# A mixer block on one core: chunk 0's gate moved behind step two of chunk 1, q loaded last, w_mod in small loads, part of every chunk's kv on GpSimd

## The chip, the cores and the metric

The kernel runs on one core of a Trainium2 chip. The metric is device time in microseconds for one execution; the median of several runs is compared. The engines of a core work in parallel, each through its own list of instructions in the order in which the kernel's text issues them, and they meet only through semaphores: TensorE (PE in the profile; PEld are its weight loads), VectorE (DVE), ScalarE (ACT), GpSimd (POOL), and SyncE (SP), which here only issues transfers. ScalarE can issue transfers too (ACTq).

## The reference

Inputs are q, k, v (2048 tokens, 640 channels, float32), a conditioning vector c, and weights.

```python
mod = (silu(c) @ w_mod).reshape(c.shape[0], 6, 1, -1)
sa, ca, ga, sb, cb, gb = ...             # six rows of 640
h = layernorm(q) * (1 + ca) + sa
# A: short causal convolution of k (4 taps), times v, long causal convolution
#    with ssm_k (2048 taps per channel, by FFT) plus ssm_D, times h
k_shift = sum of k delayed by t, times shift_k[:, 3 - t], t = 0..3
kv = k_shift * v
y = irfft(rfft(kv, 2S) * rfft(ssm_k, 2S))[:S] + kv * ssm_D
x = q + ga * (h * y)
# B: token-mixing MLP
h = layernorm(x) * (1 + cb) + sb
u = gelu(einsum("bsd,sf->bdf", h, w1) + b1)
out = x + gb * (einsum("bdf,fs->bds", u, w2) + b2).transpose
```

## The kernel before

The first part, some 290 us, does A; the rest does B, and its text is the same in both kernels. The order of all work is written out by hand: a line in the text puts an instruction at the end of its engine's list, and nothing reorders it later.

The 640 channels are taken in five chunks (c = 0..4) of 128. The long convolution is a matrix form of a Fourier transform, with these steps per chunk:

- *kv*: `kv_ops(g)` computes k_shift times v for a quarter g of the tokens: 8 elementwise instructions of 128x512 (tiles `tap`, `kt`, result in `x`). On GpSimd the same 8 instructions use the tile `t` (`PS_`, `PT`, `PW`). `kv(c_next)` gives the instructions of all quarters for VectorE, and when a quarter is done it issues the loads of k and v for the chunk after (`kv_loads`); `fill` holds them and `dv(n)` puts the next n on VectorE.
- *step one*: `step1(side, t)`, t = 0..3. 32 matmuls each (L230); ScalarE copies the result to `z` (L235). Side 0 transforms kv, side 1 transforms ssm_k. Before side 1, `perm_add` (GpSimd) adds ssm_D to one row of ssm_k as loaded by `load_ks`, and `perm` (ScalarE, L177, result in `p`) reorders it.
- *step two*: `f2(g)`, g = 0..7. 64 matmuls (L249); ScalarE copies a half (L255, `kt`), VectorE multiplies the transforms (`p<-pst,kt`, two instructions per g, into one of two halves of `P`), GpSimd adds and subtracts the products (`y<-p`, two instructions per g). In the text, the products of g - 1 and the sums of g - 2 stand behind the matmuls of g. `perm_add` of the next chunk stands behind those at g = 3.
- *back*: `i2(r)`, r = 0, 1 (L280, four copies by ScalarE, L288), and `i1(half)` (L300).
- *gate*: `a1_ops` puts the normalised q, scaled, in `A1` (half of the tile `aux`; 16 rows by ScalarE, L307, then two VectorE instructions); `gate` multiplies `A1` by y from PSUM and adds it to q in `xa`, `xb` (`XH`); `spill` stores the result to DRAM.

PSUM is a ring of three tiles of 1024 (`psum()`), so every fourth user waits until the first was read; a fourth tile, `tap`, holds VectorE's kv scratch.

Stages: chunk 0's kv; step one of both sides, then step two of chunk 0; then a stage in which chunk c goes back and is gated while step one of chunk c + 1 runs, followed by step two of chunk c + 1, and so on. The modulation rows sa, ca, ga come from w_mod (five loads of 128 x 1920 by `mod_load`, products `mod_part` in TensorE, L364, `mod_sum`, and `mod_row`, L375); three rows give `G0`, `G1`. Chunk 0's gate needs them, and needs q with its row statistics (`bn_stats`, L600, and `rstd`).

In the stage behind chunk 0's step two, SyncE's list is: the 32 q loads (already issued in step two, L532), w_mod, the constants `c_v1` of i1, chunk 1's ssm_k (`load_ks(1)`), chunk 2's k and v, `load_taps(3)`, chunk 2's ssm_k (`load_ks(2)`), the stores of chunk 0's result. The w_mod pieces 0 to 4 lie in the tiles `v`, `aux` and `p`.

The stage of chunk c = 1, 2 or 3 in the text (ScalarE's part in brackets): two step ones of side 0 [copies], `perm(c + 1)` [one instruction], 7 kv instructions, `i2(0)` [4 copies], the two VectorE instructions of `a1_ops`, `step1(0, 2)`, `i2(1)`, `step1(0, 3)`, then `i1`, gates and step one of side 1. Chunk c's 16 rows of `a1_ops` are put on ScalarE in step two, two per g.

`copy_rows` copies parts of w1 from DRAM to DRAM (`wc`) for later use in B; these ten transfers are issued in step two of chunk 3.

## Time and profile before

| what | us |
| --- | --- |
| median of 3 runs (lowest, highest) | 672.45 (670.65, 674.04) |
| the profiled execution's own time | 671.21 |
| its span, first to last instruction | 669.4 |
| step two of chunk 0 | 41.4 to 57.7 |
| stage of chunk 0 (back and gate; step one of chunk 1) | 57.7 to 105.4 |
| step two of chunk 1 | 105.4 to 126.7 |
| stage of chunk 1 | 126.7 to 156.3 |
| step two of chunk 2 | 156.3 to 172.7 |
| stage of chunk 2 | 172.7 to 201.6 |
| step two of chunk 3 | 201.6 to 220.1 |
| stage of chunk 3, step two of chunk 4, last gate and norm | 220.1 to 344 |
| part B's matmuls | 344 to 669 |

In rows of the order of time the columns are: start in us, duration in us, engine, line, operation, output<-input, partitions x elements and type, xcount (neighbouring instructions of one kind are merged), and in brackets the idle time in front with what ended it. In rows of stages: the window, its length, then busy time (and count) of PE, PEld, DVE, ACT and POOL, the granted TensorE clock as a share of full speed, the busy share of the transfer engines, and GB/s.

### The profile page before, as it was taken

Reading aid. Unit: us, or ns where it says so; the run is one execution under the profiler, and the core shown is the slowest. Engines: PE = TensorE matmul, PEld = TensorE weight load, DVE = VectorE, ACT = ScalarE, POOL = GpSimd, SP = SyncE. Lnnn points to the kernel's source line nnn. Section 1 sums busy time; section 2 is a strip of 40 time slices with the busy share of each in tenths; the row PEclk is TensorE's granted clock in tenths of the full one; section 3 lists DMA queues with packets and bytes.
Section 4 is the critical chain, followed back from the end, with each engine's and each line's share of the span. In section 5 each row is a group of like instructions: output and inputs, shape, how many; then the busy total and the mean of one; then the engine's idle time right before and its main releaser. Section 6 shows DMA issues by size and latency. Waiting matters only on the chain.

```text
span 669.4 us, 20749 instructions
## 1 busy us (share of the span) xinstructions
PE 619.5 (93%) x9073; PEld 597.8 (89%) x9073; DVE 501.9 (75%) x860; ACT 309.7 (46%) x483; POOL 108.1 (16%) x120
## 2 busy tenths in 40 slices
PE   0599878899998999999999999999999999999997
PEld 0598568788997989689999999999999999999997
DVE  6688569969969948789974213846689889888886
ACT  0574475545735647667765224334243332333331
POOL 5284027413324127000000000000000000000000
PEclk9999789999999999879999999999999999999999
DMA  9968988727438525414006630885598565345601
GB/s 179 213 194 225 391 172 159 168 54 165 83 70 221 180 51 156 172 33 95 0 1 126 119 71 1 189 234 144 174 365 268 173 179 154 102 144 169 188 31 41
DMA packets 175472, 98.01 MB, mean 146 GB/s; under 512 B 89843, under 2 KB 165398, under 8 KB 175126
## 3 DMA queue, kind: packets, MB, share of 16 engines
q1 hardware_dynamic: 170834, 95.38, 54.0%
q10 hardware_dynamic: 4548, 1.31, 1.1%
q8 instruction: 71, 1.16, 0.7%
q14 instruction: 19, 0.16, 0.1%
HBM read 79.63 MB, written 19.14 MB: 148 GB/s over the span
## 4 chain that ended last, share of the span: by engine, by line
PE 71%; DVE 16%; DMA 6%; issue 3%; SPq 2%; ACT 1%; POOL 0%; ACTq 0%; DVEq 0%; POOLq 0%
PE pst L1128 26%; PE pst L463 19%; PE pst L230 9%; PE pst L249 7%; PE pst L280 5%; PE pst L993 4%; DVE tap L60 3%; DVE kt L60 2%; DMA aux<-in_A_ssm_k_dram 2%; PE pst L300 2%; DMA aux<-in_w_mod_dram 2%; DVE p L60 1%; SPq L532 1%; PE tap L364 1%; DMA in<-in_A_k_dram 1%
## 5 line engine op out<-in xcount | busy, mean ns | idle before, releaser
L249 PE MATMUL pst<-z,w 128*64 128x64 f32 x2560 | 78.9, 223 | 11.0 <-DVE p L60 6.0
L249 PEld LDWEIGHTS pst<-z,w 128*64 128x64 f32 x2560 | 76.8, 138 | 13.7 <-issue 10.4
L230 PE MATMUL pst<-v,x 128*64 128x128 f32 x640 | 45.7, 302 | 24.2 <-DVE x L60 23.7
L230 PEld LDWEIGHTS pst<-v,x 128*64 128x64 f32 x640 | 43.6, 221 | 24.9 <-POOL t L488 23.7
L235 ACT ACTIVATE z<-pst 128x1024 f32<-128x1024 f32 (+2 forms) x45 | 41.4, 931 | 43.6 <-PE pst L230 24.9
L60 POOL TENSOR_TENSOR y<-p 128x256 f32<-128x256 f32 x72 | 54.1, 776 | 40.1 <-DVE p L60 39.7
L60 DVE TENSOR_TENSOR p<-pst,kt 128x512 f32<-128x512 f32 x80 | 50.8, 681 | 10.5 <-ACT kt L255 9.6
L280 PEld LDWEIGHTS pst<-v,y 32*128 32x128 f32 x1280 | 39.4, 193 | 4.2 <-issue 2.7
L280 PE MATMUL pst<-v,y 32*128 32x64 f32 x1280 | 41.2, 279 | 1.6 <-issue 1.0
L255 ACT ACTIVATE kt<-pst 128x512 f32<-128x512 f32 x40 | 23.9, 598 | 36.7 <-PE pst L249 20.9
L230 PE MATMUL pst<-v,p 128*64 128x128 f32 x640 | 37.3, 274 | 1.4 <-ACT p L177 1.2
L230 PEld LDWEIGHTS pst<-v,p 128*64 128x64 f32 x640 | 35.3, 137 | 2.2 <-ACT p L177 1.4
L1128 PE MATMUL pst<-r_z,m_w 128*128 128x320 f32 x198 | 37.2, 309 | 0.0
L60 DVE TENSOR_TENSOR tap<-tap,kt 128x512 f32<-128x512 f32 x51 | 35.5, 696 | 1.3
L60 DVE TENSOR_TENSOR kt<-in,tap 128x512 f32<-128x512 f32 x51 | 34.9, 685 | 1.5
L300 PEld LDWEIGHTS pst<-z,v 64*64 64x64 f32 x1280 | 24.7, 157 | 7.9 <-issue 3.5
L1128 PEld LDWEIGHTS pst<-r_z,m_w 128*128 128x128 f32 x198 | 31.1, 188 | 0.0
L300 PE MATMUL pst<-z,v 64*64 64x64 f32 x1280 | 26.9, 243 | 3.7 <-issue 2.4
L288 ACT ACTIVATE z<-pst 128x512 f32<-128x512 f32 x38 | 21.3, 664 | 18.3 <-PE pst L280 18.3
L1065 ACT ACTIVATE m_w<-m_v 128x896 fp32r<-128x896 f32 x19 | 17.9, 948 | 23.3 <-DVE m_v L60 13.0
L60 DVE TENSOR_TENSOR m_w<-m_v,m_w 128x896 fp32r<-128x896 f32 x19 | 20.6, 1086 | 6.5 <-ACT m_w L1065 6.5
L1128 PE MATMUL pst<-h_x,m_w 128*128 128x320 f32 x132 | 24.6, 309 | 0.0
(303 smaller groups left out, 1417.2 us busy)
## 6 DMA issues: line engine op xcount, KB each, us to landing
x<-in_B_w_dram SPq DMA_DIRECT2D x18, 512.0 KB
m_v<-in_B_w_dram SPq DMA_DIRECT2D x20, 384.0 KB
aux<-in_A_ssm_k_dram SPq DMA_DIRECT2D x10, 512.0 KB
out_dram<-m_w SPq DMA_DIRECT2D x32, 160.0 KB
in<-in_A_k_dram SPq DMA_DIRECT2D x36, 128.0 KB
in<-in_A_v_dram SPq DMA_DIRECT2D x36, 128.0 KB
ts<-m_p SPq DMA_DIRECT2D x10, 320.0 KB
m_w<-xs SPq DMA_DIRECT2D x20, 160.0 KB
```

Source lines behind the costliest of these rows:

```text
L60: TT = lambda eng, o, a, b, op: eng.tensor_tensor(o, a, b, op=op)
L230: pe.matmul(ps.rearrange("p (b m a) -> p b a m", b=2, a=4)[64 * ri:64 * ri + 64, a // 4, a % 4], lhs, F1[:, 128 * ri:128 * ri + 128], star ...
L235: act.activation(Z[:, side, t, :, k0:k1], ps.rearrange("p (b k a) -> p b k a", b=4, a=4)[:, :, k0:k1], AF.Copy)
L249: pe.matmul(pk[64 * h:64 * h + 64, kk // 4, ri, kk % 4], W2[k1 // 32][:, 2 * (k1 % 32) + ri], rhs, start=True, stop=True)
L255: act.activation(halves_(kt), pv[:, :, 1], AF.Copy)
L280: pe.matmul(pp[qd // 2][:, o:o + 64], Y[p, ri, i:i + 2].rearrange("p i k -> p (i k)"), V2[p, 64 * ri:64 * ri + 64], start=ri == 0, stop=ri ...
L288: act.activation(o, i, AF.Copy)
L300: pe.matmul(ps[64 * b:64 * b + 64, 512 * e + 64 * jj:512 * e + 64 * jj + 64], V1[p, ri, n2], T2[p, :, 32 * ri + n2], start=ri == 0, stop=r ...
L463: pe.matmul(ps[0:m, h, 0:320], w_.bitcast(F32R), r_[:, 320 * h:320 * h + 320].bitcast(F32R), start=first and i == 0, stop=last and i == 2)
L993: pe.matmul(ps[n][:, h, 0:320], sets[n][:, j].bitcast(F32R), r[:, 320 * h:320 * h + 320].bitcast(F32R), start=j == 0 and r is hh, stop=j = ...
L1065: act.activation(W[n][0].bitcast(F32R), A[p, w_], AF.Copy)
L1128: pe.matmul(bank[n], w[:, i].bitcast(F32R), r.bitcast(F32R), start=m == 0 and k == 0, stop=m == 6 and k == 2)
```

## The change

1. *w_mod in small loads, early.* Pieces 0 to 2 go, as 18 loads of 64 x 640 (`mod_gently`), into `xa` and the front of `xb`, where q will lie later; they and `c_v1` are issued ahead of step one of chunk 0. Pieces 3 and 4 go into the rest of `xb`, behind the loads of chunk 2's k and v.
2. *q last.* The 32 loads of q are issued behind the five w_mod products, `xb` first. The statistics: five rows by VectorE ahead of chunk 1's side-1 step one, then, in step two of chunk 1 from g = 2, one row by VectorE (`q_stats`) and one by ScalarE (`q_moments`) per g. SyncE's list is now: w_mod (part), k and v of chunk 2, w_mod (rest), `load_ks(1)`, q, k and v of chunk 3, `load_ks(2)`.
3. *Chunk 0's gate behind step two of chunk 1.* In the stage of chunk 0, ScalarE stores y from PSUM in `aux` where `A1` lies. In the stage of chunk 1 come `rstd`, 16 rows by ScalarE (`late_rows`, into the tiles `t` and `kt`), three VectorE instructions and a GpSimd add per half (`late_gate`), the store of chunk 0, and then all 16 rows of chunk 1's `a1_ops` at once (`run(ac)`).
4. *kv.* In the stage of chunk 0, VectorE runs its three quarters of chunk 2's kv at once, in place of spreading them over step two of chunk 1. In the stages of chunks 1 and 2, quarter 2 of the next kv goes to GpSimd: seven instructions at the front, the last behind `step1(0, 3)`. VectorE has 24 instructions there in place of 32.
5. *Row copies.* They are issued at the ends of the stages of chunks 1 and 2.
6. *Tap loads* for chunks 2 and 3 are issued by ScalarE.

The diff, cut to its core:

```diff
+    def mod_gently(kk, place):
+        for j in range(3):
+            for b in range(2):
+                sync.dma_start(place[j][64 * b:64 * b + 64],
+                               dram(w_mod, (128 * kk + 64 * b) * 6 * D + 640 * j, [[6 * D, 64], [1, 640]]))
...
     all_taps()
-    load_taps(2)
+    xab = [XR(j) for j in range(8)] + [T_x[1][:, 0:640]]
+    pl = [xab[0:3], xab[3:6], xab[6:9]] + [...]
+    sync.dma_start(T_v1[:, 0:4096], c_v1, max_dma_last_dim=4096)
+    for kk in range(3):
+        mod_gently(kk, pl[kk])
...
+    def q_moments(j):
+        act.activation(T_t[:, 0:640], XR(j), AF.Identity, scale=1 / D, accum_out=mv[:, j, 0:1])
+        act.activation(tm[:, j:j + 1], mv[:, j, 0:1], AF.Copy, scale=-D ** -0.5)
+        act.activation(T_t[:, 640:1280], XR(j), AF.Square, scale=D ** -0.5, bias=tm[:, j:j + 1],
+                       accum_out=mv[:, j, 1:2])
+    def late_rows(half):
+        for i in range(8):
+            j = 8 * half + i
+            act.activation(G_[half][:, i], XR(j, 0, DC), AF.Identity, scale=rs1[:, j:j + 1], bias=nm1[:, j:j + 1])
+    def late_gate(half):
+        a = G_[half]
+        g = lambda G: G[:, None, 0:DC].to_broadcast([128, 8, DC])
+        TT(dve, a, a, g(G1), ALU.mult)
+        TT(dve, a, a, g(G0), ALU.add)
+        av = a.rearrange("p j (m e) -> p e j m", e=2)
+        y = T_aux[:, 2048 + 1024 * half:3072 + 1024 * half]
+        TT(dve, av, y.rearrange("p (e j m) -> p e j m", e=2, j=8), av, ALU.mult)
+        x = XH[half][:, :, 0:DC]
+        TT(pool, x, x, a, ALU.add)
...
-            if c:
+            if c > 1:
                 n_ = 2 if cn is not None else 3
                 for f_ in ac[n_ * g:n_ * g + n_]:
                     f_()
-            if cn == NC - 1:
-                copy_rows(2, g % 2, g // 2, 1)
-                if g in (3, 6):
-                    copy_rows(3, g // 6)
...
             if c == 0 and g < 4:
                 lay_w2(1, g)
-                if g == 3:
-                    load_q()
+                if g == 1:
+                    load_taps(2, act)
+            if c == 1 and g > 1:
+                q_stats(QJ[2 * g + 1])
+                if g < 7:
+                    q_moments(QJ[2 * g + 2])
...
             if c and cn is not None and g == 3:
                 perm_add(cn)
...
         if c == 0:
+            pool.tensor_scalar(PW, TR.rearrange("p (i s) -> p s i", s=4), 1.0, None, op0=ALU.mult)
+            taps()
+            load_taps(3, act)
             load_k(2, 1)
...
             load_v(2, 3)
+            for kk in (3, 4):
+                mod_load(0, kk, T_x[1][:, 1920 * kk - 4480:1920 * kk - 2560])
+            load_ks(1)
+            for t in range(4):
+                step1(0, t)
             perm_add(1)
             run(kv_ops(2, pool))
+            ps = psum()
+            pe.transpose(ps[:, 0:36], stg, ID[0:36, 0:36])
+            act.activation(cols, ps[:, 0:36], AF.Copy)
+            act.activation(sil, cols[:, 30:35], AF.Silu)
+            i2(0)
+            i2(1)
+            ps = psum()
+            for kk in range(5):
+                mod_part(ps, kk, pl[kk])
+            load_q()
+            mod_sum(ps, T_kt[:, 0:640])
             perm(1)
+            ops = kv(3, ((0,), (1, 2), (3,)))
+            run(ops)
             load_ks(2)
         elif cn is not None:
+            if c == 1:
+                rstd(rs1, nm1, 0, 16)
+            step1(0, 0)
+            if c == 1:
+                late_rows(0)
+            step1(0, 1)
+            if c == 1:
+                late_rows(1)
+                for half in range(2):
+                    late_gate(half)
+                spill(0)
+                run(ac)
             perm(cn)
             if c + 2 < NC:
-                fill.extend(kv(c + 3 if c + 3 < NC else None))
+                pool_ops = kv_ops(2, pool)
+                run(pool_ops[:-1])
+                fill.extend(kv(c + 3 if c + 3 < NC else None, ((0,), (1, 2), (3,))))
...
             step1(0, 3)
+            if cn < NC - 1:
+                run(pool_ops[-1:])
             dv(3 if cn < NC - 1 else 28)
...
         for half in range(2):
             ps = i1(half)
+            if c == 0:
+                act.activation(T_aux[:, 2048 + 1024 * half:3072 + 1024 * half], ps, AF.Copy)
+                if half:
+                    for i in range(3):
+                        mod_row(i, T_kt[:, 0:640])
+                    for j in QJ[0:5]:
+                        q_stats(j)
+                continue
...
+        if c:
+            spill(c)
+        if c in (1, 2):
+            for n in range(4):
+                copy_rows(2, n % 2, 2 * (c - 1) + n // 2, 1)
+            copy_rows(3, c - 1)
```

More of the change, by code (lines that the diff above doesn't have):

```diff
@@ L526, in mixer_kernel, with q_stats @@
     three = lambda t: [t[:, 640 * j:640 * j + 640] for j in range(3)]
[L527 removed]
+    QJ = (*range(8, 16), *range(8))
     def load_q():
[L530 removed]
+        for j in QJ:
             for b in range(2):
                 sync.dma_start(XH[j // 8][64 * b:64 * b + 64, j % 8], dram(q, (16 * b + j) * D, [[32 * D, 64], [1, D]]))
[L533 to L534 removed]
+    def q_stats(j):
+        for h in range(2):
+            dve.bn_stats(bst[:, j, h, :], XR(j, 320 * h, 320))
+        dve.bn_aggr(mv[:, j, :], bst[:, j, 0:2, :])
+    def q_moments(j):
[3 more added lines that the diff above has]
+                       accum_out=mv[:, j, 1:2])
+    G_ = [t[:, 0:1024].rearrange("p (j d) -> p j d", j=8) for t in (T_t, T_kt)]
+    def late_rows(half):
[12 more added lines that the diff above has]
+        TT(pool, x, x, a, ALU.add)
     fill = kv_ops(3)
@@ L606, in mixer_kernel @@
         if c == 0:
-            mod_load(0, 4, P[:, 0:1920])
-            for t in range(4):
-                step1(0, t)
-            ps = psum()
-            pe.transpose(ps[:, 0:36], stg, ID[0:36, 0:36])
-            act.activation(cols, ps[:, 0:36], AF.Copy)
-            act.activation(sil, cols[:, 30:35], AF.Silu)
-            i2(0)
-            for kk in range(4):
-                mod_part(tap, kk, pl[kk])
-                if kk == 1:
-                    sync.dma_start(T_v1[:, 0:4096], c_v1, max_dma_last_dim=4096)
-                if kk == 2:
-                    load_ks(1)
-            rstd(rs1, nm1, 0, 16)
-            run(ac[0:4])
-            i2(1)
-            mod_part(tap, 4, pl[4])
+            pool.tensor_scalar(PW, TR.rearrange("p (i s) -> p s i", s=4), 1.0, None, op0=ALU.mult)
+            taps()
+            load_taps(3, act)
             load_k(2, 1)
@@ L719, in mixer_kernel @@
             fill.extend(x1s(c, j) for j in range(16))
-        else:
-            dv(11 if c else 8)
+        elif c:
+            dv(11)
     r_z, r_v = mem("z", 8192, "r_z"), mem("v", 4520, "r_v")
```

27 lines of the change are left out of this document (2 added, 25 removed).

## The prediction

> **What bounds the kernel now.** I read the page's busy shares first, then busy time by stage, then the order of time of each engine and queue between 36 and 160 us, where every edit lies. The page:
>
> ```profile
> PE 619.5 (93%) x9073; PEld 597.8 (89%) x9073; DVE 501.9 (75%) x860; ACT 309.7 (46%) x483; POOL 108.1 (16%) x120
> ```
>
> TensorE is the bound over the whole span. Stages (window; its length; PE, PEld, DVE, ACT, POOL busy; clock; DMA):
>
> ```profile
> 72.00:78.00 6.00, 5.01 (x33) 1.55 (x36) 5.15 (x18) 3.32 (x6) 1.35 (x2) 0.62 1.04 400
> 105.40:126.70 21.30, 16.39 (x512) 15.69 (x513) 20.79 (x34) 10.31 (x23) 12.14 (x16) 1.00 0.79 161
> 126.70:156.30 29.60, 28.41 (x769) 26.95 (x769) 23.13 (x32) 15.95 (x22) 6.94 (x6) 1.00 0.50 98
> 156.30:172.70 16.40, 15.57 (x511) 15.23 (x513) 16.16 (x27) 10.29 (x22) 8.95 (x14) 1.00 0.59 140
> 201.60:220.10 18.50, 15.91 (x512) 15.46 (x513) 16.71 (x27) 10.28 (x22) 9.58 (x15) 1.00 0.84 239
> ```
>
> Step two of chunk 1 (105.4 to 126.7) is held by VectorE, busy 20.79 of 21.30. The stage behind it (126.7 to 156.3) has TensorE at 28.41 of 29.60: there is next to nothing to win, and whatever is put in front of TensorE there is lost. Steps two of chunks 2 and 3 could give at most 0.8 and 2.6 us (length less PE busy). From chunk 4 on the text is unchanged, so the question is when chunk 1's stage ends.
>
> **SyncE's queue.** In the new order the q loads wait for the third w_mod product, because q overwrites the tiles in which w_mod lies. TensorE, in order of time (start, duration):
>
> ```profile
> 57.71 8.29 PE L230 MATMUL pst<-v,x 128*64 128x128 f32 x128
> 67.13 4.80 PE L280 MATMUL pst<-v,y 32*128 32x64 f32 x124 [0.58 <-ACT z L235]
> 72.55 4.40 PE L364 MATMUL tap<-v,sm 128*32 128x320 f32 x24 [0.63 <-DMA v<-in_w_mod_dram]
> 84.81 1.28 PE L364 MATMUL tap<-p,sm 128*32 128x320 f32 x12
> 97.51 7.51 PE L230 MATMUL pst<-v,p 128*64 128x128 f32 x128 [1.24 <-ACT p L177]
> 130.95 3.80 PE L280 MATMUL pst<-v,y 32*128 32x64 f32 x128
> 136.91 4.04 PE L280 MATMUL pst<-v,y 32*128 32x64 f32 x128
> 143.13 2.10 PE L300 MATMUL pst<-z,v 64*64 64x64 f32 x128
> 156.30 5.82 PE L249 MATMUL pst<-z,w 128*64 128x64 f32 x192 [0.44 <-ACT z L235]
> ```
>
> ScalarE:
>
> ```profile
> 73.74 1.28 ACT L348 ACT_TABLE_LOAD   x1
> 90.27 3.18 ACT L307 ACTIVATE aux<-xb,sm 128x128 f32<-128x128 f32 x8
> 131.05 1.02 ACT L235 ACTIVATE z<-pst 128x1024 f32<-128x1024 f32 x1 [1.00 <-PE pst L230]
> 131.97 2.08 ACT L177 ACTIVATE p<-aux 128x2048 f32<-128x2048 f32 x1
> 134.78 2.33 ACT L288 ACTIVATE z<-pst 128x512 f32<-128x512 f32 x4 [0.72 <-PE pst L280]
> ```
>
> Step one of chunk 1 ends at 66.0 as before; i2(0) runs 67.13 to 71.93; i2(1) needs the first two of i2(0)'s four copies (2.33 for four), so from 73.1 for 3.80 to 76.9; three w_mod products at 1.28 end at 80.7. There load_q may start. What stands behind it is priced by SyncE's rows
>
> ```profile
> 41.81 11.35 SPq L532 DMA_DIRECT2D xa<-in_A_q_dram  x16
> 53.20 11.97 SPq L532 DMA_DIRECT2D xb<-in_A_q_dram  x16
> 78.72 10.23 SPq L167 DMA_DIRECT2D aux<-in_A_ssm_k_dram  x2
> 105.09 0.71 SPq L165 DMA_DIRECT2D rows<-in_A_ssm_D_dram  x2
> 105.85 4.13 SPq L167 DMA_DIRECT2D aux<-in_A_ssm_k_dram  x2
> 128.01 1.27 SPq L151 DMA_DIRECT2D in<-in_A_v_dram  x2
> ```
>
> and by GpSimd's:
>
> ```profile
> 94.48 0.77 POOL L60 TENSOR_TENSOR aux<-aux,rows 1x64 f32<-1x64 f32 x1 [3.31 <-issue]
> 101.69 2.14 POOL L60 TENSOR_TENSOR t<-in,t 128x512 f32<-128x512 f32 x1
> 105.27 1.28 POOL L60 TENSOR_TENSOR t<-in,t 128x512 f32<-128x512 f32 x1
> 111.25 1.42 POOL L60 TENSOR_TENSOR y<-p 128x256 f32<-128x256 f32 x2 [1.96 <-DVE p L60]
> 115.87 0.78 POOL L60 TENSOR_TENSOR aux<-aux,rows 1x64 f32<-1x64 f32 x2
> ```
>
> q: 32 issues, 11.35 + 11.97 = 23.3, to 104.0. Chunk 3's k and v, which the text puts behind q: 18 issues at 0.64 = 11.5, to 115.5. ssm_D 0.71, to 116.2. Only then comes chunk 2's ssm_k. Before, that load was issued at 105.85 and was there when GpSimd wanted it at 115.87, so it takes at most 10.0; at least its own issue, 4.13; and 15.8 in the stage where it left at 78.72 and the second half's add ran at 94.48, behind other large loads. I take 9: near the row of this very load, the queue in front being k and v then as now. It lands at 125.2.
>
> **GpSimd waits for it inside step two.** The row at 115.87 is perm_add(2), written in step two of chunk 1 behind the sums of group 1, and the change leaves it there. GpSimd works in order, so the sums of groups 2 and up stand behind it until T = 125.2 + 0.8 = 126.0. The products of group 4 need the P half that the sums of group 2 read; f2(7) needs the PSUM of group 4. TensorE comes early to this point: five w_mod products end at 83.3, then two i1 (2.10 each), the rows of the gate (some 1.4, estimated as one w_mod product of as many matmuls) and step one of ssm_k (7.51) end near 96.4, so step two starts 9.0 earlier than 105.4. Seven groups then run to about 112, and TensorE stops. The 9 us won are spent waiting; the term in the sum is T alone.
>
> After T, VectorE has sums to wait for and its own list:
>
> ```profile
> 59.88 0.88 DVE L600 BATCH_NORM_STATS2 sm<-xa 128x6 f32<-128x320 f32 x2
> 60.80 0.21 DVE L601 BATCH_NORM_AGGREGATE sm<-sm 128x2 f32<-128x12 f32 x1
> 76.39 0.26 DVE L339 RECIPROCAL sm<-sm 128x16 f32<-128x16 f32 x1 [0.38 <-ACT sm L348]
> 77.69 0.18 DVE L353 SCALAR_TENSOR_TENSOR sm<-sm 128x16 f32<-128x16 f32 x1
> 91.41 4.92 DVE L60 TENSOR_TENSOR aux<-aux,g 128x1024 f32<-128x1024 f32 x4
> 98.51 1.97 DVE L60 TENSOR_TENSOR xa<-xa,aux 128x1024 f32<-128x1024 f32 x1
> 110.49 1.28 DVE L60 TENSOR_TENSOR p<-pst,kt 128x512 f32<-128x512 f32 x2
> 128.88 0.89 DVE L60 TENSOR_TENSOR y<-p 128x128 f32<-128x128 f32 x4
> 189.24 0.69 DVE L60 TENSOR_TENSOR x<-tap,in 128x512 f32<-128x512 f32 x1 [3.94 <-PE pst L230]
> ```
>
> Sums 1.42, four pairs of products (4 x 1.28), three rows of q statistics (3 x 1.05), y sums 0.89: T + 10.6. The root's Newton steps (76.39 to 77.87, 1.5) end at T + 12.1.
>
> **ScalarE's queue in chunk 1's stage.** The copies of i2(0) stand behind all of the late gate's rows. From T + 12.1: late_rows(0) 3.2, a step-one copy 1.0, late_rows(1) 3.2, to 19.5. Chunk 1's own 16 rows overwrite the stored y, so the second eight wait for late_gate(1): three VectorE passes of 1.23 behind 19.5, one of them beside GpSimd (0.7 more), to 23.9; eight rows 3.2 to 27.1; perm(2) 2.1 to 29.2; the four copies 2.3 to 31.5. The table load and root lie before T + 12.1, beside VectorE's list; bare, they would cost 1.6. Meanwhile i2(0) itself could run at T + 10.6 and TensorE has one step one besides; then it stands. So i2(1) starts at T + 31.5 = 157.5, where it started at 136.91: **20.6 later**.
>
> **Smaller parts.** From i2(1) on the order to step two of chunk 2 is as before (136.91 to 156.30). TensorE restarts after a stop of over 10 us: 24 w_mod matmuls took 4.40 where the clock was 0.62, against 2 x 1.28; I take 1.5 for a slow start, bounds 0 and 4. (The Trainium skill, TensorE: Matmul & The Clock Gate, Part 1, says that an idle window of some 3.4 us halves the clock until about 3.4 us of work have passed; by it an estimate of the loss is 1.7 us, and the sum would be 0.2 higher. The 0.62 agrees.) Fill moved from VectorE to GpSimd: step two of chunk 2 gains 0.8 (all of its gap); chunk 3's, with the row copies out too, up to 2.6, of which I take 1.7, the rest of the gap being fetch waits that may stay. The w_mod loads in halves (18 issues of q's shape, 0.7 each, on an else free SyncE from 38) and chunk 2's k, v, ssm_k behind them are through before 81 and cost nothing; if ssm_k of chunk 1 took 15.8 again from about 66, perm(1) would still be ready near 85, before step one at 88.9. The two tap loads moved to ScalarE delay a copy by at most 1.2 in front of i2: taken as 0, bound 1.2. ScalarE's q moments (two passes of 640 and a small one, estimated 1.5 from the 1.02 for 1024) lie in the wait, or else beside VectorE's 2.3 per group.
>
> GpSimd's kv part runs beside chunk passes of VectorE: the same 1024-wide pass took 1.97 beside GpSimd and 1.23 alone, GpSimd's op 2.14 and 1.28. The scaling by the gate (2 x 2.3) so grows by up to 3.5; VectorE idles 3.94 right behind it in chunk 2 and is not late in chunk 1, so 0; without that cover, 3.5 per chunk. (The Trainium skill, SBUF — State Buffer, SBUF: two separate sides, has one holder of the shared port pair for a whole instruction; by it, as an estimate, each pass waits for one GpSimd op, together 2.6 per chunk, hidden too. The two rows agree with it in kind.)
>
> **Sum:** +20.6 + 1.5 - 0.8 - 1.7 = +19.6. The profiled execution took 671.21 (span 669.4), so 690.8; the median, 672.45, lies 1.2 higher. I forecast 691. T's bounds are 121.1 (load at its issue) and 132.8 (load as at 78.72); with the clock's and the taps' this one case has 684 to 701.
>
> **Rivals.**
> *The load is in time* (no loss). GpSimd doesn't stand at perm_add(2) if T is at most 106: step two at VectorE's pace would then end as if T were 106.0, i2(1) would start at 137.5, and the sum is +0.6 + 1.5 - 2.5: 672. It decides there, and each us of T beyond is one us of time. For it speaks that TensorE and VectorE are free 9 us earlier; against it that 32 + 18 + 4 issues cannot leave SyncE in 10 us, where they took 35. Chance 0.08.
> *Only that wait bites*: i2(0)'s copies find ScalarE free. i2(1) then follows i2(0) by 5.96 as in the rows, T + 16.6 = 142.6, +5.7 - 2.5: 675. Against it stands the order of the text. 0.09.
> *Neither bites*, and the first stage's gain is kept: 106.0 + 16.6 = 122.6, -14.3 - 2.5: 655. 0.04.
> *More is late*: chunk 3's k and v or ssm_k, issued behind all this, hold step two of chunk 2 again, or the lock shows on the path: 5 to 12 more, about 702. 0.10.
> The forecast has 0.69.
>
> **Numbers.** No change means within 0.5%, 3.4 us, about what a measurement of this kernel can tell. Slower: 0.69 + 0.10 + half of the second rival; same: the first rival and most of that half; faster: the third, and a little of the first. Range 677 to 702: below lie the first three rivals, about 0.2.
>
> **What would show it.** In step two of chunk 1 a TensorE hole of over 10 us ending with GpSimd's sums, GpSimd idle until an ssm_k load; SyncE issuing q from about 81 to 104 and that load near 116; then a second hole of some 12 us between step one and i2, its releaser ScalarE; a lower clock behind both. Wrong if GpSimd's one-row add has no wait (T small), or if z copies of i2 follow TensorE at once. Steps two of chunks 2 and 3 should be 15.5 to 17 us long.

## The result, and the profile after

The change makes the kernel slower: 707.89 us (median of 4 runs, 704.86 to 715.97) against 672.48 for the kernel before on the same chip (4 runs), a ratio of 1.0566 with a 95% interval of 1.0507 to 1.0624. The profiled execution took 704.86, its span is 703.1 us (669.4 before), the mean granted clock 0.958 (0.982). Forecast were 691, and 677 to 702 as the range. Medians in this document are over all executions, while the ratios leave out executions of a slower state (here the one of 715.97) and can differ from the quotient of the medians (1.0527 here).

The page's busy shares:

```profile
PE 624.7 (89%) x9073; PEld 603.6 (86%) x9073; DVE 491.4 (70%) x827; ACT 319.9 (46%) x510; POOL 137.3 (20%) x140
```

TensorE has the same 9073 instructions and is busy 5.2 us longer (619.5 before), at the lower clock; the other 28.5 of the 33.7 us are, on balance, added stops.

TensorE in order of time, changed kernel (columns as before). The lines are step two of chunk 1, the stage behind it, and the starts of steps two of chunks 2, 3 and 4:

```profile
110.41 4.19 PE L249 MATMUL pst<-z,w 128*64 128x64 f32 x136 [0.44 <-ACT z L235]
141.95 3.68 PE L249 MATMUL pst<-z,w 128*64 128x64 f32 x64 [16.71 <-DVE p L60]
169.69 0.69 PE L280 MATMUL pst<-v,y 32*128 32x64 f32 x4 [12.92 <-ACT z L288]
170.69 7.09 PE L280 MATMUL pst<-v,y 32*128 32x64 f32 x124 [0.31 <-ACT z L288]
192.91 15.39 PE L249 MATMUL pst<-z,w 128*64 128x64 f32 x511 [0.44 <-ACT z L235]
237.69 11.48 PE L249 MATMUL pst<-z,w 128*64 128x64 f32 x378 [0.44 <-ACT z L235]
251.78 5.67 PE L249 MATMUL pst<-z,w 128*64 128x64 f32 x133 [2.61 <-issue]
287.13 15.15 PE L249 MATMUL pst<-z,w 128*64 128x64 f32 x512 [0.44 <-ACT z L235]
```

There are the two holes that were forecast, 16.71 and 12.92 us, where the kernel before had five short ones in step two of chunk 1, the longest 1.17. What ends them is seen on GpSimd and VectorE (first hole) and on ScalarE (second hole):

```profile
136.24 0.34 POOL L60 TENSOR_TENSOR aux<-aux,rows 1x64 f32<-1x64 f32 x1 [18.94 <-DMA aux<-in_A_ssm_k_dram]
139.25 0.35 POOL L60 TENSOR_TENSOR aux<-aux,rows 1x64 f32<-1x64 f32 x1 [2.66 <-issue]
140.43 1.37 DVE L60 TENSOR_TENSOR p<-pst,kt 128x512 f32<-128x512 f32 x2 [18.01 <-POOL y L60]
```

```profile
150.31 3.19 ACT L561 ACTIVATE t<-xa,sm 128x128 f32<-128x128 f32 x8 [0.49 <-DVE sm L353]
154.31 3.18 ACT L561 ACTIVATE kt<-xb,sm 128x128 f32<-128x128 f32 x8
157.39 3.18 ACT L307 ACTIVATE aux<-xa,sm 128x128 f32<-128x128 f32 x8
163.49 3.19 ACT L307 ACTIVATE aux<-xb,sm 128x128 f32<-128x128 f32 x8 [2.92 <-DVE kt L60]
166.58 2.06 ACT L177 ACTIVATE p<-aux 128x2048 f32<-128x2048 f32 x1
168.53 2.10 ACT L288 ACTIVATE z<-pst 128x512 f32<-128x512 f32 x4
```

GpSimd stands 18.94 us in front of perm_add(2) until chunk 2's ssm_k has landed; T, the end of that add, is 139.60. VectorE, which needs GpSimd's sums, goes on at 140.43, and TensorE behind it at 141.95. ScalarE then works through late rows, chunk 1's own rows and perm(2) before it copies i2(0) out (L288 at 168.53). i2(1) gets through four matmuls at 169.69 and the other 124 from 170.69 = T + 31.1; the latter is called its start here. The mechanism is the forecast's, and so is its second term, T + 31.5. T itself was to be 126.0. SyncE's queue shows why it isn't:

```profile
38.85 27.15 SPq L363 DMA_DIRECT2D xa<-in_w_mod_dram  x16
82.92 7.03 SPq L167 DMA_DIRECT2D aux<-in_A_ssm_k_dram  x2
90.05 15.31 SPq L543 DMA_DIRECT2D xb<-in_A_q_dram  x16
105.41 11.10 SPq L543 DMA_DIRECT2D xa<-in_A_q_dram  x16
131.61 3.24 SPq L167 DMA_DIRECT2D aux<-in_A_ssm_k_dram  x2
```

Sixteen w_mod loads, taken as 0.7 each, kept the queue for 27.15 us. The queue's own waits between 30 and 140 us (line, what for, us in total, times, longest):

```profile
SPq L363 <- DMA rows<-in_A_shift_k_dram: 11.3, 2, 9.0
SPq L363 <- DMA v<-in_const_v_dram: 3.6, 1, 3.6
SPq L363 <- DMA g<-in_B_b_dram: 2.9, 2, 2.6
```

A load of w_mod into `xa` waits for a load of the taps into `rows`: neither data nor buffer have to do with each other, and the tap load stands in another engine's queue. In the trace's events, eight completion semaphores are used in turn by all transfers of SyncE and ScalarE: a transfer's instruction waits on the very semaphore that it is to signal, so it stands until the one that had this semaphore last has landed. A turn of eight is short while the loads are small and quick to issue, so one late landing anywhere in it (taps 9.0, `c_v1` 3.6, the b rows 2.6) stops the queue.

The tap loads that held SyncE for 9.0 us, from 55.9 to 64.9, were not slow themselves. They had not been issued:

```profile
60.53 1.12 POOL L641 TENSOR_SCALAR t<-rows 128x256 f32<-128x256 f32 x1
61.68 1.12 ACTq L161 DMA_DIRECT2D rows<-in_A_shift_k_dram  x2
62.85 2.86 ACT L235 ACTIVATE z<-pst 128x1024 f32<-128x1024 f32 x3 [4.02 <-issue]
```

They overwrite `rows`, so they left only at 61.68, when GpSimd had read it. ScalarE, in whose list they came next, stood 4.02 us in front of them, and SyncE stood for the semaphore that the first of them was to use. The kernel before had a wait of this kind too, 3.0 us of a tap load for a table of constants in `xb`; the line stood in its profile, and the prediction made nothing of it.

The account, profiled execution against profiled execution (starts of the L280 and L249 rows above against those before):

| stretch | before | after | change | forecast |
|---|---|---|---|---|
| up to i2(1) of chunk 1 | 136.91 | 170.69 | +33.8 | +20.6 |
| i2(1) to step two of chunk 2 | 19.39 | 22.22 | +2.8 | +1.5 |
| to step two of chunk 3 | 45.28 | 44.78 | -0.5 | -0.8 |
| to step two of chunk 4 | 48.68 | 49.44 | +0.8 | -1.7 |
| to the end, unchanged text | 419.14 | 415.97 | -3.2 | 0 |
| span | 669.4 | 703.1 | +33.7 | +19.6 |

The last row but one is luck of this execution: the same text took between 415.6 and 420.2 in the others shown here.

### The profile page after: what moved, and what is told of

It is laid out like the page before. It is cut to its first block, busy times and chain, and to the rows that moved or that the text cites. A ratio compares the mean times of both kernels' runs of the same rounds, so it can differ in the third digit from the quotient of the medians.

```text
span 703.1 us, 20790 instructions
## 1 busy us (share of the span) xinstructions
PE 624.7 (89%) x9073; PEld 603.6 (86%) x9073; DVE 491.4 (70%) x827; ACT 319.9 (46%) x510; POOL 137.3 (20%) x140
## 4 chain that ended last, share of the span: by engine, by line
PE 73%; DVE 12%; DMA 4%; ACT 3%; SPq 3%; issue 3%; POOL 1%; ACTq 0%; DVEq 0%; POOLq 0%
PE pst L1179 25%; PE pst L469 18%; PE pst L230 10%; PE pst L249 10%; PE pst L280 4%; PE pst L1044 3%; DMA aux<-in_A_ssm_k_dram 2%; PE pst L300 2%; DVE kt L60 2%; SPq L151 1%; DMA in<-in_A_k_dram 1%; DVE tap L60 1%; SPq L145 1%; DVE p L60 1%; DVE xb L833 1%
## 5 line engine op out<-in xcount | busy, mean ns | idle before, releaser
L249 PE MATMUL pst<-z,w 128*64 128x64 f32 x2560 | 81.0, 227 | 24.8 <-DVE p L60 16.7
L249 PEld LDWEIGHTS pst<-z,w 128*64 128x64 f32 x2560 | 79.2, 142 | 26.3 <-issue 22.8
L230 PE MATMUL pst<-v,x 128*64 128x128 f32 x640 | 46.4, 304 | 24.4 <-DVE x L60 23.3
L230 PEld LDWEIGHTS pst<-v,x 128*64 128x64 f32 x640 | 44.2, 220 | 26.1 <-POOL t L494 23.3
L280 PE MATMUL pst<-v,y 32*128 32x64 f32 x1280 | 44.8, 292 | 15.9 <-ACT z L288 14.2
L280 PEld LDWEIGHTS pst<-v,y 32*128 32x128 f32 x1280 | 42.9, 206 | 18.3 <-ACT z L288 14.8
L255 ACT ACTIVATE kt<-pst 128x512 f32<-128x512 f32 x40 | 23.9, 597 | 48.2 <-PE pst L249 19.3
L230 PE MATMUL pst<-v,p 128*64 128x128 f32 x640 | 38.4, 281 | 0.0
L230 PEld LDWEIGHTS pst<-v,p 128*64 128x64 f32 x640 | 36.5, 142 | 0.8 <-ACT g L390 0.4
L60 DVE TENSOR_TENSOR tap<-tap,kt 128x512 f32<-128x512 f32 x45 | 31.4, 698 | 1.4
L60 DVE TENSOR_TENSOR kt<-in,tap 128x512 f32<-128x512 f32 x45 | 30.9, 687 | 1.4
L1179 PEld LDWEIGHTS pst<-r_z,m_w 128*128 128x128 f32 x198 | 31.1, 188 | 0.0
L60 POOL TENSOR_TENSOR t<-in,t 128x512 f32<-128x512 f32 x20 | 27.3, 1375 | 14.9 <-DMA in<-in_A_k_dram 13.9
L288 ACT ACTIVATE z<-pst 128x512 f32<-128x512 f32 x38 | 21.1, 650 | 19.9 <-PE pst L280 19.8
L60 DVE TENSOR_TENSOR tap<-in,tap 128x512 f32<-128x512 f32 x15 | 10.4, 694 | 23.7 <-DMA in<-in_A_k_dram 23.3
L300 PEld LDWEIGHTS pst<-z,v 64*64 64x64 f32 x1280 | 21.9, 142 | 5.0 <-issue 2.3
L948 ACT ACTIVATE pst<-pst,sm 128x640 f32<-128x640 f32 x14 | 10.7, 765 | 33.4 <-PE pst L469 33.4
```

The source lines that it names most:

```text
L60: TT = lambda eng, o, a, b, op: eng.tensor_tensor(o, a, b, op=op)
L230: pe.matmul(ps.rearrange("p (b m a) -> p b a m", b=2, a=4)[64 * ri:64 * ri + 64, a // 4, a % 4], lhs, F1[:, 128 * ri:128 * ri + 128], star ...
L249: pe.matmul(pk[64 * h:64 * h + 64, kk // 4, ri, kk % 4], W2[k1 // 32][:, 2 * (k1 % 32) + ri], rhs, start=True, stop=True)
L255: act.activation(halves_(kt), pv[:, :, 1], AF.Copy)
L280: pe.matmul(pp[qd // 2][:, o:o + 64], Y[p, ri, i:i + 2].rearrange("p i k -> p (i k)"), V2[p, 64 * ri:64 * ri + 64], start=ri == 0, stop=ri ...
L288: act.activation(o, i, AF.Copy)
```

## The experiments

Ratios are to the kernel before on the same chip, with a 95% interval; T, i2(1) and holes are from each run's own trace.

**Only the tap loads' place** (e12_taps3_later). ScalarE issues chunk 3's taps later in its own queue; no instruction of SyncE changes.

```diff
-            load_taps(3, act)
...
             perm(1)
+            load_taps(3, act)
```

> The changed kernel with one pair of loads moved within ScalarE's own queue: the taps of chunk 3 are issued behind perm(1), when w_mod's small loads are done, instead of right behind the conversions of chunk 2's taps. No instruction of SyncE changes. Theory (SyncE's w_mod loads stood 9.0 us for the completion of exactly these two loads of another queue into another buffer): SyncE's wait of 9.0 for the shift_k load is gone, w_mod's loads are through at 56 to 60 instead of 67.3, ssm_k's issue of chunk 1 at 79 to 84 instead of 90, q starts at 84 to 86 where the products allow it, perm_add(2) ends at 134 to 136, time 701 to 704. Rival 1 (the next late transfer holds them instead, as c_v1 did for 7.6 where the taps went to SyncE): q starts at 86 to 89, time 704 to 706. Rival 2 (the wait is the DMA engines' own and only shows against the taps): w_mod's loads still end near 67, 706 to 709.

Measured: 698.10, ratio 1.0409 (1.0340 to 1.0478). SyncE's queue and its waits in this run:

```profile
39.01 17.50 SPq L363 DMA_DIRECT2D xa<-in_w_mod_dram  x16
74.10 8.31 SPq L167 DMA_DIRECT2D aux<-in_A_ssm_k_dram  x2
84.70 13.45 SPq L543 DMA_DIRECT2D xb<-in_A_q_dram  x16
SPq L543 <- PE pst L370: 2.2, 1, 2.2
SPq L363 <- DMA rows<-in_A_shift_k_dram: 1.9, 1, 1.9
```

The wait of 9.0 is gone, w_mod's loads take 9.7 us less, and q starts at 84.70, where now the w_mod product (PE L370) releases it, as the forecast had it. The four executions that keep these loads in their place (the changed kernel, e6, e1 and e2 below) have q start at 89.39 to 90.68. T is 132.1, i2(1) starts at 163.18, both somewhat better than expected, and the interval of the ratio lies below that of the changed kernel. Two loads in the queue of another engine held SyncE. That is shown; both rivals fall, though `c_v1` (4.0) and the b rows (2.7) still hold the queue for less.

**Taps on SyncE** (e3_taps_sync), one pair ahead of w_mod, one behind chunk 2's k and v.

```diff
     all_taps()
+    load_taps(2)
...
-                if g == 1:
-                    load_taps(2, act)
...
-            load_taps(3, act)
...
             load_v(2, 3)
+            load_taps(3)
```

> The changed kernel with the tap loads of chunks 2 and 3 back on SyncE: chunk 2's ahead of the constants and w_mod, chunk 3's behind chunk 2's k and v. Theory (w_mod's small loads are slow to leave because each transfer waits until the transfer that last used its completion semaphore has landed, SyncE and ScalarE share eight of them in turn, and ScalarE's tap load, itself waiting for GpSimd, holds two: 9.0 and 2.3 us): SyncE issues the 18 w_mod loads from about 42 to 57 in place of 38.9 to 67.3, chunk 2's k and v and ssm_k follow 9 to 11 earlier, the fourth w_mod product no longer waits (3.8 and 1.4), q starts at about 81 to 83 in place of 90, and the end of perm_add(2), with it the time, comes 6 to 9 earlier: 696 to 699. Rival (the transfer engines are busy, each small load takes its time): SyncE still needs 25 us or more for them and time does not change. Rival (q's start is set by ssm_k's own issue of 7.0 ahead of it): SyncE is early, but q starts later than 86 and less than 4 us are won.

Measured: 701.70, ratio 1.0500 (1.0437 to 1.0563). The taps no longer appear among w_mod's waits, but `c_v1` now holds a semaphore of the turn:

```profile
SPq L363 <- DMA v<-in_const_v_dram: 7.6, 1, 7.6
```

w_mod's loads are through at 61.0 and q starts at 86.24, behind the issue of chunk 1's ssm_k (8.87 us from 77.27), which is the second rival's outcome. i2(1) starts at 164.92. The ratio's interval overlaps that of the changed kernel, so the times alone show no gain.

**Few large loads** (e5_few_loads): w_mod's pieces 0 to 2 in four loads.

```diff
-    for kk in range(3):
-        mod_gently(kk, pl[kk])
+    for kk in range(2):
+        mod_load(0, kk, T_x[0][:, 1920 * kk:1920 * kk + 1920])
+    sync.dma_start(T_x[0][:, 3840:5120], dram(w_mod, 256 * 6 * D, [[6 * D, 128], [1, 1280]]), ...)
+    sync.dma_start(T_x[1][:, 0:640], dram(w_mod, 256 * 6 * D + 1280, [[6 * D, 128], [1, 640]]))
```

> The changed kernel with the first three w_mod pieces in four large loads instead of 18 small ones. Theory (each transfer of SyncE waits until the transfer that last used its completion semaphore has landed, so 18 small loads stand where four do not): these loads leave SyncE within 3 us of 39 instead of 28.4, chunk 2's k and v follow near 62 (bound by their buffers) and ssm_k's issue ends near 84; q starts at 82 to 85 instead of 90.05, the end of perm_add(2) comes at 132 to 135 instead of 139.7, and the time is 700 to 704 on a chip where the changed kernel has about 706. Rival 1 (the stall only moves to the next transfers, since the late holder is the same): q starts at 88 to 91 and the time is 705 to 709. Rival 2 (large loads take the DMA engines from step two of chunk 0): a fetch wait of over 2 us in that stage, step two of chunk 0 later by 2 to 5, 706 to 712.

Measured: 700.88, ratio 1.0521 (1.0493 to 1.0548). The four loads left between 38.35 and 45.6, but the stall went to the next in the queue, chunk 2's k and v:

```profile
SPq L151 <- DMA rows<-in_A_shift_k_dram: 11.0, 1, 11.0
SPq L145 <- DMA rows<-in_A_shift_k_dram: 6.0, 1, 6.0
```

q still started at 85.61, held by the product. So the first rival's mechanism appeared, and the theory's numbers came about all the same (q's start is 0.6 late), since the first w_mod loads had left 22 us earlier (45.6 against 67.3). T is 133.0, i2(1) 164.12. Here too the interval of the ratio overlaps that of the changed kernel.

**ssm_k ahead of chunk 3's k and v** (e6_ssm_k_first).

```diff
+            load_ks(2)
             run(ops)
-            load_ks(2)
```

> The changed kernel with chunk 2's ssm_D and ssm_k issued right behind q, ahead of chunk 3's k and v; nothing else moves. It tests the rule of the sum that each us by which perm_add(2) ends earlier is one us of time. Theory: the load leaves near 118, lands near 125, perm_add(2) ends at 125 to 127 instead of 139.7, i2(1) at 156 to 158 instead of 170.7, and the time is 692 to 696. Rival 1 (behind the wait the ten-odd moments of q on ScalarE pace step two, as they did where the add stood behind the late gate): i2(1) gains only 9 to 11, time 697 to 700. Rival 2 (issue of ssm_k next to q is slow, 7 to 10 us, landing 12 to 16): perm_add(2) near 132, time 699 to 702.

Measured: 696.33, ratio 1.0440 (1.0398 to 1.0482). The load leaves at 117.60, and

```profile
125.87 0.35 POOL L60 TENSOR_TENSOR aux<-aux,rows 1x64 f32<-1x64 f32 x1 [1.89 <-DMA aux<-in_A_ssm_k_dram]
128.58 3.63 PE L249 MATMUL pst<-z,w 128*64 128x64 f32 x64 [3.17 <-DVE p L60]
156.32 0.69 PE L280 MATMUL pst<-v,y 32*128 32x64 f32 x4 [12.97 <-ACT z L288]
157.32 7.09 PE L280 MATMUL pst<-v,y 32*128 32x64 f32 x124 [0.31 <-ACT z L288]
```

T = 126.2, by accident nearly the forecast's T; the hole in step two shrinks to 3.17, the one ahead of i2 stays at 12.97. Five runs with five T now stand beside each other:

| | T | i2(1) starts | difference |
|---|---|---|---|
| changed kernel | 139.60 | 170.69 | 31.1 |
| e3_taps_sync | 133.83 | 164.92 | 31.1 |
| e5_few_loads | 133.02 | 164.12 | 31.1 |
| e12_taps3_later | 132.09 | 163.18 | 31.1 |
| e6_ssm_k_first | 126.22 | 157.32 | 31.1 |

One us of T is one us at i2(1). In the time a part of it is lost again: here 13.4 at i2(1) came to 6.8 in the span, since the stretches of the account above took 23.7, 46.0, 50.1 and 419.2 (22.2, 44.8, 49.4 and 416.0 in the changed kernel's execution). Half of what is lost, 3.2, lies in the unchanged tail, which was short by luck there.

**The add behind the late gate** (e1_add_behind): perm_add(2) directly ahead of perm(2), no longer in step two of chunk 1.

```diff
-            if c and cn is not None and g == 3:
+            if c > 1 and cn is not None and g == 3:
                 perm_add(cn)
...
+                perm_add(cn)
             perm(cn)
```

> The changed kernel with one edit: chunk 2's perm_add stands behind step two of chunk 1, directly ahead of perm(2), and no longer in step two at g = 3. First theory (GpSimd's sums stand behind perm_add(2), which waits for a late ssm_k, and each us of that wait is one us of time): the 16.7 us hole of TensorE in step two of chunk 1 goes, VectorE (8 pairs of products at 1.29, 6 statistics of 1.05, y sums 0.9 from 113.3 on) ends that step at about 131 where it ended at 149.2, GpSimd still waits for ssm_k until about 139 but under ScalarE's rows, so time falls by 16 to 19, to 686 to 690. Rival (q is late, and its statistics hold VectorE and ScalarE): the hole stays, because the statistics of the last q rows still wait, and time stays within 4 us of 705. Rival (the transfers themselves are short of rate): the wait goes over to perm(2), which then stands until after 150, and less than 8 us are won.

Measured: 693.89, ratio 1.0388 (1.0317 to 1.0460).

```profile
125.56 3.77 PE L249 MATMUL pst<-z,w 128*64 128x64 f32 x122 [0.35 <-issue]
154.50 0.69 PE L280 MATMUL pst<-v,y 32*128 32x64 f32 x4 [11.61 <-ACT z L288]
155.52 7.09 PE L280 MATMUL pst<-v,y 32*128 32x64 f32 x124 [0.33 <-ACT z L288]
```

The first hole is gone (step two of chunk 1 runs from 112.38 to 129.3 without a stop over 0.5), the second remains, i2(1) gains 15.2. The span gains 10.3; the rest is lost behind i2(1), 2.7 of it in the unchanged tail (418.7), so the time is 4 above the expectation.

**No late gate in the changed kernel** (e2_no_late_gate): the rows and the gate are left out, and chunk 0 goes out ungated.

```diff
-            if c == 1:
-                late_rows(0)
             step1(0, 1)
             if c == 1:
-                late_rows(1)
-                for half in range(2):
-                    late_gate(half)
                 spill(0)
                 run(ac)
```

> The changed kernel without chunk 0's late gate: the 16 rows on ScalarE, the six VectorE instructions and the two GpSimd adds are left out (chunk 0's q goes out ungated); chunk 1's 16 rows stay where they are. Theory (the second hole is ScalarE's queue: i2(0)'s copies stand behind both sets of rows and behind the wait of chunk 1's second eight rows for the late gate): two times 3.18 of rows and the wait of 2.9 go, so i2(0)'s copies begin about 9.3 earlier (18 to 19 us behind the first product after perm_add in place of 28), the hole of 12.9 shrinks to 3 or 4 but is not gone, since chunk 1's own rows (6.4) and perm (2.1) still stand ahead; with a little from the clock time falls by 9 to 12, to 693 to 696. Rival (TensorE is held there by GpSimd's kv part and the shared port): the hole stays and less than 3 us are won. Rival (the whole stage is paid by the clock): as much is won, but i2(1)'s matmuls alone account for it.

Measured: 699.59, ratio 1.0470 (1.0405 to 1.0535). T was 136.6 here, 3.0 earlier, although the two texts agree up to there: so much can T differ between executions.

```profile
159.49 0.69 PE L280 MATMUL pst<-v,y 32*128 32x64 f32 x4 [6.28 <-ACT z L288]
```

i2(1) started at 160.50, T + 23.9 instead of T + 31.1: the late gate is 7.2 of it, and of the second hole 6.28 remain, with chunk 1's sixteen rows and perm(2) in front of the copies. The expectation had asked for more: 9.3 instead of 7.2, a hole of 3 or 4, and 693 to 696.

**All three mended** (e7_all_mended): e1's edit; e5's loads, with `c_v1` behind them and both tap loads on SyncE; and on ScalarE, in chunk 1's stage, this order:

```diff
+            step1(0, 1)
+                late_rows(0)
+                dv(7)
+                i2(0)
+                late_rows(1)
+                for half in range(2):
+                    late_gate(half)
+                spill(0)
+                step1(0, 2)
+                run(ac[0:8])
+                i2(1)
+                run(ac[8:16])
+                step1(0, 3)
+                perm_add(cn)
             perm(cn)
```

> The changed kernel with all three suspected losses taken away: perm_add(2) behind the late gate; w_mod's first three pieces in four large loads, c_v1 behind them, both tap loads on SyncE (so nothing of ScalarE's queue stands in their way); and on ScalarE, in chunk 1's stage, the copies of i2 ahead of the second late rows and of chunk 1's own sixteen. Theory (the added time is those two holes of TensorE and the late start of q, nothing else): step two of chunk 1 starts at 96 to 100 and ends at 116 to 120, no hole of over 4 us ahead of i2(1), which starts at 131 to 137 (136.9 in the kernel before), and the time is 664 to 672, i.e. no worse than 0.5% above the kernel before. Rival (the late gate is work that the stage cannot hide: 16 rows on ScalarE at 0.4, six VectorE passes of 1.2 to 2.4): i2(1) near 140, step two of chunk 2 another 4 to 6 later, 674 to 682.

Measured: 676.95 (6 runs), ratio 1.0159 (1.0134 to 1.0185). Some seven tenths of the loss are mended, (1.0566 - 1.0159) / 0.0566 = 0.72; it is still slower than before.

```profile
130.63 3.96 PE L280 MATMUL pst<-v,y 32*128 32x64 f32 x128
139.88 2.10 PE L300 MATMUL pst<-z,v 64*64 64x64 f32 x128 [2.83 <-ACT z L288]
145.82 3.47 PE L230 MATMUL pst<-v,p 128*64 128x128 f32 x32 [3.84 <-ACT p L177]
153.12 5.46 PE L230 MATMUL pst<-v,p 128*64 128x128 f32 x96 [1.80 <-DVE aux L60]
159.01 5.82 PE L249 MATMUL pst<-z,w 128*64 128x64 f32 x192 [0.43 <-ACT z L235]
```

i2(1) starts 6.3 earlier than in the kernel before (130.63 against 136.91): that is what the change could win. But step two of chunk 2 follows it by 28.4 us instead of 19.4, with three new holes of 2.83, 3.84 and 1.80. The theory's places were right up to i2(1), its 664 to 672 was not. The rival, that this stage can't hide the work put into it, had the time right (674 to 682) but not the places: it put i2(1) near 140, and step two of chunk 2 another 4 to 6 later where it is 9.0.

**The mended kernel without the late gate** (e10_mended_no_gate): e7 less the calls of `late_rows` and `late_gate`, as in the diff of e2.

> The mended kernel (add behind the late gate, few w_mod loads, taps on SyncE, copies of i2 early) without the late rows and the late gate: chunk 0 goes out ungated, that work is done nowhere. It measures what the late gate's work costs where no order is against it. In the mended kernel i2(1) started 6.3 us earlier than in the kernel before (130.63 against 136.91), but step two of chunk 2 followed it by 28.4 instead of 19.4. Theory (these 9 us are the late gate: 8.4 us of VectorE passes and 6.4 of ScalarE rows in front of chunk 1's own rows, scaling and gate): i2(1) at 128 to 131, step two of chunk 2 19 to 21 behind it, time 660 to 666. Rival (the 9 us are GpSimd's kv part beside VectorE's scaling by the gate, which took 6.42 instead of 4.61, and waits of ScalarE's order): step two of chunk 2 is still 25 to 28 behind i2(1), time 671 to 676.

Measured: 673.64, ratio 1.0103 (1.0061 to 1.0146).

```profile
137.16 3.86 PE L280 MATMUL pst<-v,y 32*128 32x64 f32 x128
149.46 3.68 PE L230 MATMUL pst<-v,p 128*64 128x128 f32 x32 [3.83 <-ACT p L177]
161.96 11.54 PE L249 MATMUL pst<-z,w 128*64 128x64 f32 x388 [0.44 <-ACT z L235]
```

Step two of chunk 2 comes 24.8 behind i2(1). The theory's 19 to 21 fails; the rival's time came (671 to 676), and its 25 to 28 all but. Of the 9.0 us the late gate is 3.6, and 5.4 stay without it. The hole ahead of L230 that perm(2) ends is as long as with the gate: on ScalarE perm(2) stands behind chunk 1's sixteen rows (3.18 and 3.19), which the kernel before ran two by two inside step two of chunk 1, where they were hidden, and which can't start before q's statistics. That these rows are the whole 5.4 was not tried by itself.

The ratios differ by 0.0056, 3.7 us, with intervals that overlap; that this is so near 3.6 is chance. In this execution i2(1) lies 6.5 later than in e7: 2.5 is there when chunk 0's i2 begins (72.04 against 69.50), 2.1 more comes from that i2 at a lower clock (7.09 against 4.95), 1.7 from step one of ssm_k (8.87 against 7.21). What follows the start of step two of chunk 2 is 5.2 shorter.

**GpSimd's part and the row copies.** The mended kernel with VectorE doing all four quarters, as before the change (e11_mended_no_pool):

```diff
-                pool_ops = kv_ops(2, pool)
-                run(pool_ops[:-1])
-                fill.extend(kv(c + 3 if c + 3 < NC else None, ((0,), (1, 2), (3,))))
+                fill.extend(kv(c + 3 if c + 3 < NC else None))
...
-            if cn < NC - 1:
-                run(pool_ops[-1:])
```

> The mended kernel with the late gate, but without GpSimd's part of the kv work in chunks 1 and 2 (VectorE does all four quarters, as in the kernel before). It measures what the shared use costs and gains in this stage. Theory (VectorE fills the stretch between i2(1) and step two of chunk 2; eight passes of 0.69 come back to it, about 2.8 us of slower passes beside GpSimd go): stage and steps two of chunks 2 and 3 together change by -1 to +3, step two of chunks 2 and 3 each 1 longer with VectorE as releaser again, time 676 to 680 where the mended kernel had 677. Rival (GpSimd's part is the loss: late gate and scaling on VectorE double beside it): step two of chunk 2 comes 3 to 5 earlier, time 671 to 674.

Measured: 679.33, ratio 1.0156 (1.0084 to 1.0229), against 1.0159 with GpSimd's part: no difference that these runs can tell, with an interval of some 10 us. And on the kernel before, the row copies alone (e4_copies_only, 12 runs; the edit shown) and these with the lines above put in (e9_before_copies_pool, 12 runs):

```diff
-            if cn == NC - 1:
-                copy_rows(2, g % 2, g // 2, 1)
-                if g in (3, 6):
-                    copy_rows(3, g // 6)
...
         spill(c)
+        if c in (1, 2):
+            for n in range(4):
+                copy_rows(2, n % 2, 2 * (c - 1) + n // 2, 1)
+            copy_rows(3, c - 1)
```

> The kernel before with one part of the change alone: the ten row copies go from step two of chunk 3 to the ends of the stages of chunks 1 and 2. Theory (the fetch waits of TensorE in that step, 1.76, come with the copies' traffic): step two of chunk 3 falls from 18.5 to 16.5 or less, time by 1 to 2.5. Rival (the fetch waits come without them as well; the changed kernel had 2.6 in the same step): the wait stays or moves, time within 1 us of before, or up to 1 us slower by the copies' traffic beside k and v.

> The kernel before with two parts of the change only: GpSimd takes quarter 2 of the k and v work in the stages of chunks 1 and 2, and the row copies stand behind the gate of chunks 1 and 2 instead of in step two of chunk 3. Theory (both are gains of their own, hidden in the change by the late gate): step two of chunk 2 is 0.5 to 1 shorter, that of chunk 3 1.5 to 2.5 (the copies alone made it about 1 shorter), time 0.993 to 0.998 of the kernel before. Rival 1 (no gain beyond the copies'): 0.996 to 1.000. Rival 2 (GpSimd's passes beside VectorE's chunk-wide ones double both, which shows on the path): 1.002 to 1.008.

Measured: copies 666.91, ratio 0.9968 (0.9931 to 1.0005); both 669.35, ratio 1.0001 (0.9970 to 1.0033). In the second of them, steps two of chunks 2 and 3:

```profile
154.66 15.43 PE L249 MATMUL pst<-z,w 128*64 128x64 f32 x511 [0.44 <-ACT z L235]
198.58 11.41 PE L249 MATMUL pst<-z,w 128*64 128x64 f32 x382 [0.44 <-ACT z L235]
211.93 5.63 PE L249 MATMUL pst<-z,w 128*64 128x64 f32 x130 [1.94 <-issue]
```

VectorE's gaps are gone from both (chunk 2's took 16.6 from first start to last end, now 15.5). In chunk 3 a stop of 1.94 stays, which the profile puts down to no engine ("issue"); the prediction calls such stops fetch waits. Five of the ten copies still run at the start of this step: they are issued at its edge, from 197.91 to 202.10 here and from 237.99 to 241.61 in the changed kernel. So this run doesn't show the step without copies. e4 comes nearer: its transfer engines are idle from 210 to 214 (share 0.02), so the copies have landed, and a stop of 0.97 still comes at 218.5, with loads of w_mod under way (share 0.91). Neither part is a gain that these runs can tell from nothing, so none of these kernels is shown to beat the kernel before.

## Why the prediction was wrong, point by point

- *Direction and mechanism* were right: perm_add(2) waits in step two of chunk 1, then ScalarE's late rows hold i2, and everything behind is shifted.
- *T + 31.5 for i2(1)*: 31.1 in five runs, in part because two errors offset each other. Newton ends at 150.3, T + 10.7 (T + 12.1 forecast). The late rows are 3.19 and 3.18 (3.2), but the late gate's second pair of passes, beside GpSimd, takes 4.67 where the first takes 2.48 (0.7 more was forecast). Chunk 1's second eight rows so start at T + 23.9, as forecast.
- *T = 126.0 is the step that failed*: 139.6, above its own bound of 132.8. The term in it is "the w_mod loads in halves ... 0.7 each, on an else free SyncE ... through before 81 and cost nothing". Sixteen took 27.15 instead of 11.2; with them late, chunk 1's ssm_k was still in issue until 89.95 and q started 9.3 later than forecast (90.05 against 80.7). q took 26.6 to the next load's issue instead of 23.3 and chunk 3's k and v 14.1 instead of 11.5, 5.9 together; from ssm_D to the end of the add it was 1.6 less. 9.3 + 5.9 - 1.6 = 13.6. Priced by q's rows in a stretch without such waits, the issue times were a lower end, and I gave them no upper one. e12 gives the share of the tap loads: q starts 5.4 earlier and T is 7.5 earlier, of which up to 3.0 may be the difference between executions that e2 shows. What is left there against 126.0, 6.1, is 4.0 for q's start (i2 and the first products at half clock), 1.8 and 2.1 for the issues, less 1.8 behind them.
- *The sum*: 691 adds the 19.6 to the profiled execution; added to the median it is 692.
- *The clock*, 1.5 forecast with 0 to 4: i2(1) took 7.09 instead of 4.04 and the step one behind it 3.19 instead of 2.28, 4.0 lost, of which 2.8 is left at step two of chunk 2. The upper bound, not the value taken. "The 0.62 agrees" was a misreading: in the kernel before TensorE had no long stop in front of that window (0.58 and 0.63 in the rows at 67.13 and 72.55).
- *Steps two of chunks 2 and 3*: 16.1 us in chunk 2 (15.6 forecast); in chunk 3 19.6 (16.8), with a stop of 2.61. The term -1.7 took most of that stop for something that goes with the copies. It did not go: half of the copies are still issued at the start of that step, and in e4 a stop comes after they have landed. What causes it was not tried.
- *The taps on ScalarE*, "taken as 0, bound 1.2", were priced by the copy that they delay on ScalarE. ScalarE stood 4.02 us for them, above the bound, but i2(0) began only 0.2 late (67.36 against 67.13). By way of SyncE's queue they cost some 4.5 to 7.5 us of T.
- *GpSimd's part hidden*: e11 and e9 find no difference; they would not see less than some 3 us.
- *Rivals*: "more is late" (about 702) came nearest, not by its mechanism: neither k and v nor ssm_k held step two of chunk 2.

## What to carry to other kernels

Price a queue of loads not only by issue times and by what they wait for in the program: look in the queue's waits for transfers that wait for another transfer with which they share no data. A late landing anywhere in the turn, whichever engine issues that transfer and however late it can leave, gives the upper end of the price. A wait inside an in-order queue is worth its whole length once nothing else is left in front of the bound engine: here each us of T was a us at i2(1), in five runs. And work that was hidden between the groups of a step has a price when it moves behind it: the stage that took in the sixteen rows and the gate grew by 9.0 us even in the best order tried (3.6 of it the gate; the rows' share was not tried by itself), more than the 6.3 us that the early start had won.

## What the runs showed of the hardware

A lower clock needs no long stop here, and a busy TensorE does not end it at once. Stretches of the changed kernel behind the second hole (window; length; busy time of the engines; clock), then of e5 in chunk 0's stage:

```profile
169.70:173.70 4.00, 3.69 (x60) 3.50 (x64) 3.97 (x2) 1.84 (x3) 3.92 (x2) 0.50 0.04 12
173.70:177.70 4.00, 4.00 (x76) 3.89 (x72) 0.19 (x1) 0.27 (x1) 3.84 (x3) 0.50 0.00 0
```

```profile
70.00:74.00 4.00, 2.97 (x100) 2.84 (x100) 2.48 (x4) 1.90 (x6) 0.00 (x0) 0.94 0.86 193
74.00:78.00 4.00, 4.00 (x84) 4.00 (x80) 3.76 (x6) 0.55 (x2) 0.00 (x0) 0.50 0.85 206
```

The Trainium skill (TensorE: Matmul & The Clock Gate, Part 1) has, in its table of the two states, the clock return after about 3.4 us of sustained work and fall after an idle window of that length. Here it stayed at 0.50 through some 8 us of work, 4.00 busy of 4.00 in the second line, and it fell to 0.50 in e5 after stops of 0.57 and 1.03 us, none longer since 60 us. Both times the work was i2, matmuls with 32 rows of the array; whether that is why was not tried.

The other surprise is the turn of completion semaphores, a wait that stands in the program's own instructions: two loads of taps, 64 KB each, stopped another engine's queue for 9.0 us, and for four of these the transfer engines moved nothing (0 GB/s between 58 and 62 us).
